# Attention, two feed-forward stages and one core: a new table of task times for the list scheduler of the attention stage

## The chip, the cores and the metric

One core of a Trainium2 chip runs the whole program in one launch. The metric is the device time of one execution, in microseconds. TensorE (PE) does the matmuls and the transposes, VectorE (DVE), ScalarE (ACT) and GpSimd (POOL) the arithmetic between them, SyncE (SP) issues most DMAs, ACT's queue a few.

## The reference, cut to what matters

```python
p_packed = sm_attn(p, k, v)            # 32 packed rows per head attend to 576 keys
out = sm_attn(q, p_packed, p_packed)   # 576 queries per head attend to the 32 packed rows
x = out.transpose(0, 2, 1, 3).reshape(B * S, H * D)      # 4608 tokens x 512
x = moe(x)     # 8 experts, the best one per token: relu(x @ w1[e]) @ w2[e], times its gate
return moe2(x) # h = x @ w_in (512 x 2048); silu(h) @ w_out
```

There are 8 batches of 8 heads, 576 positions and a head size of 64; everything is float32.

## The kernel before, in words

The program has three stages one after the other: `attention` (which also computes the first expert layer of batch 0), `experts`, and `ffn`. The change touches only the order of the first.

`attention` writes no instruction directly. It describes operations (`Sched.op`): an engine, a cost in the model, what it reads and writes, and the task that it belongs to. `Sched.run` then sorts all operations by the time of their task in the table `TIMES` (plus the operation's place within the task), looks at the first `window` operations of what is left, and takes the one that can start soonest by the model's costs; on a tie the one that stands earlier. It does this until nothing is left, and emits the instructions in that order. Each engine runs its own instructions in exactly the order emitted. DMA issues on SP keep the order in which `attention` names them; their rank is below everything.

The tasks are named by a letter, a batch b and a part:

- `k` (b, t): transposes of the keys (`ktp`, L1624, and `krp`, L1611) and of the packed rows (`ptp`, L1598), then the scores `s1p` (L1638, L1643), maximum on DVE, exponent on ACT.
- `p` (b, t): the exponents are transposed (`e1p`, `e1rp`, L1665 and L1671), multiplied by the values (`ppp`, L1690), scaled, transposed again (`pptp`, L1698); `mp` (L1716, L1719) are small products for the router.
- `q` (b, r): queries are transposed (`qtp`, L1736, which reads the tile `qm`), their scores are `s2p` (L1753), then the softmax on DVE, ACT and POOL. r is 0 or 1; part 2 of an odd batch is the rest of two batches (`qs`, L1819, L1828).
- `x` (b, r): the weights are transposed (`a2p`, L1776, L1849), stored to DRAM from ACT's queue, and multiplied with `mp` for the router's logits (`xp`, L1790, L1860).
- `r` (u): the routing of two batches, with the small product `cnt` (L389, L390).
- `m`: the first expert layer of batch 0. Part 0 loads the expert's weights `w1c` (2 MiB, L467) and the stored attention `af`; parts 1 and 2 multiply the packed rows with them (`m0p`, L506); parts 3 to 10 are eight products `a0p` (L541), each followed by a relu on ACT (L544) and the low half on DVE (L548). `m0p` and `a0p` all write the one PSUM buffer with the tag `s1`, which the scores `s1p` use before them: a product can start only when ACT and DVE have read the one before.
- `d`: a copy on POOL that doubles the packed rows.

Loads of keys (`km` 1 MiB, `kr` 128 KiB), values (`vm`, `vr`) and queries (`qm`, and `qs` for odd batches) have two buffers each. So the load of batch b's queries waits until all transposes of batch b-2's queries are done, and as SP's order is fixed, every load behind it in SP's queue waits with it. SP's order after the first batches is: keys of b+2, queries of b+1, values of b+2, packed rows of b+3, keys of b+3 and so on; the 2 MiB of `w1c` come behind the last queries.

When the last operation of the stage has been emitted, `experts` follows, whose first PE instruction is at L600; L620 is its second layer.

## Time and profile before

| | us |
|---|---|
| median of 3 runs | 1213.74 (1213.04 to 1214.96) |
| the profiled execution, its own time | 1214.78 |
| its span | 1212.9 |
| PE busy | 1173.9 (97% of the span) |
| DVE, ACT, POOL busy | 876.9, 526.4, 146.9 |
| attention stage, until PE reaches L600 | 0 to 178.37 |

The span is the time from the first to the last instruction that the profiler saw; some 2 us of the execution lie around it. A time in a row is counted from the start of the span. A busy PE is a PE that has a matmul in flight; as matmuls overlap, the next row's start says more about the length of a group than its own duration does.

### The profile page before, as it was taken

To read this page: it belongs to the slowest core of one execution; us is meant where nothing else is said; L and a number is where in the kernel's file an instruction comes from. 1 tells how busy PE (TensorE), PEld (TensorE's weight loads), DVE (VectorE), ACT (ScalarE), POOL (GpSimd) and SP (SyncE) were. 2 spreads that over 40 slices of the span, in tenths; PEclk is the share of its full clock that TensorE was granted. 3 is DMA by queue.
4 is the path that set the end of the run, shared out by engine and by line. 5 is a ranking of instruction groups with operands and counts; after the bars stand their busy time and mean duration, and the time that the engine had idled before them with its cause. 6 is when DMAs were issued, how large, how long until landed. Compare 5 with 4: busy or idle time off the path is not lost.

```text
span 1212.9 us, 24417 instructions
## 1 busy us (share of the span) xinstructions
PE 1173.9 (97%) x9548; PEld 1034.1 (85%) x9549; DVE 876.9 (72%) x1560; ACT 526.4 (43%) x911; POOL 146.9 (12%) x259
## 2 busy tenths in 40 slices
PE   8788899999999999999999999999999999999998
PEld 7676679999989998978878878889998888888887
DVE  5475877886897883586765585634878888888886
ACT  4565652333343233464445354434643333333342
POOL 3222220221132432100000000002000000000000
PEclk9999999999999999999999999999999999999999
DMA  9979657569668965576876745788855657575652
GB/s 260 258 222 264 213 184 248 189 245 336 248 233 297 341 209 164 168 231 194 312 253 200 233 142 147 229 260 259 273 212 173 189 176 216 161 221 164 208 145 49
DMA packets 228313, 264.62 MB, mean 218 GB/s; under 512 B 32024, under 2 KB 181784, under 8 KB 227680
## 3 DMA queue, kind: packets, MB, share of 16 engines
q1 hardware_dynamic: 213192, 230.66, 59.2%
q0 software_dynamic: 8048, 27.53, 8.4%
q10 hardware_dynamic: 6952, 4.80, 1.3%
q8 instruction: 77, 1.26, 0.4%
q14 instruction: 44, 0.36, 0.1%
HBM read 175.26 MB, written 87.69 MB: 217 GB/s over the span
## 4 chain that ended last, share of the span: by engine, by line
PE 56%; DVE 3%; issue 1%; ACT 1%; DMA 0%; SPq 0%; DVEq 0%; ACTq 0%
PE p L1202 17%; PE p L1200 10%; PE p L906 8%; PE p L908 8%; PE p L907 8%; PE ps L620 2%; DVE x L899 1%; PE p L1205 1%; PE p L1204 1%; PE ps L541 1%; DVE raw L899 0%; DMA raw<-y_d 0%; DVE mh L899 0%; DMA c_d<-x 0%; DVE y L899 0%
## 5 line engine op out<-in xcount | busy, mean ns | idle before, releaser
L899 DVE TENSOR_TENSOR x<-p,x 128x512 f32<-128x512 f32 (+1 forms) x148 | 90.2, 619 | 58.8 <-PE p L908 52.8
L940 ACT ACTIVATE x<-x 128x512 f32<-128x512 f32 (+1 forms) x111 | 66.7, 603 | 137.5 <-DVE x L899 125.5
L620 PE MATMUL ps<-hkm,w2s 128*128 128x288 f32 x768 | 123.5, 296 | 0.0
L620 PEld LDWEIGHTS ps<-hkm,w2s 128*128 128x128 f32 x768 | 108.5, 188 | 5.9 <-DVE cu L678 1.7
L541 PE MATMUL ps<-at,mh 128*128 128x288 f32 x672 | 93.1, 297 | 4.2 <-PEq L735 2.1
L541 PEld LDWEIGHTS ps<-at,mh 128*128 128x128 f32 x672 | 90.5, 188 | 5.4 <-issue 3.5
L1202 PE MATMUL p<-x,x 128*128 128x512 f32 x332 | 90.4, 394 | 0.0
L620 PE MATMUL ps<-hvm,w2s 128*128 128x288 f32 x448 | 85.3, 295 | 0.0
L1202 PEld LDWEIGHTS p<-x,x 128*128 128x128 f32 x332 | 62.7, 189 | 10.8
L620 PEld LDWEIGHTS ps<-hvm,w2s 128*128 128x128 f32 x448 | 68.3, 188 | 0.1
L899 DVE TENSOR_TENSOR x<-p,y 128x512 f32<-128x512 f32 (+1 forms) x57 | 33.1, 581 | 42.8 <-PE p L908 39.1
L899 DVE TENSOR_TENSOR y<-p,y 128x256 f32<-128x256 f32 (+1 forms) x71 | 34.5, 485 | 35.4 <-PE p L1200 27.3
L1169 ACT CAST x<-rawe 128x1024 fp32r<-128x1024 f32 x35 | 36.4, 1051 | 49.5 <-DVE rawe L899 49.5
L620 PE MATMUL ps<-hqm,w2s 128*128 128x288 f32 x320 | 52.7, 294 | 0.0
L544 ACT ACTIVATE hkm<-ps 128x576 fp32r<-128x576 f32 x42 | 27.3, 652 | 55.7 <-PE ps L541 50.0
L630 ACT COPY yb<-ps 128x576 f32<-128x576 f32 x20 | 12.8, 642 | 88.3 <-PE ps L620 84.8
L1202 PE MATMUL p<-t,x 128*128 128x512 f32 x166 | 51.1, 389 | 0.0
L1187 POOL DMA_DIRECT2D x<-c_d x14 | 12.1, 865 | 319.8 <-DMA x<-c_d 223.1
L620 PEld LDWEIGHTS ps<-hqm,w2s 128*128 128x128 f32 x320 | 46.0, 188 | 0.0
L906 PE MATMUL p<-x,t 128*128 128x512 f32 x112 | 43.9, 392 | 1.5 <-DVE x L899 1.0
L591 DVE TENSOR_TENSOR w2s<-w2c,w2s 128x1024 fp32r<-128x1024 f32 x32 | 40.1, 1252 | 7.2 <-ACT w2s L588 7.2
L1222 ACT COPY raw<-p 128x256 f32<-128x256 f32 x18 | 6.7, 373 | 86.4 <-PE p L1200 86.4
(442 smaller groups left out, 3235.1 us busy)
## 6 DMA issues: line engine op xcount, KB each, us to landing
c_d<-x SPq DMA_DIRECT2D x136, 256.0 KB, 2.9
raww1c<-c_d SPq DMA_DIRECT2D x36, 512.0 KB, 6.1
rawe<-c_d SPq DMA_DIRECT2D x36, 512.0 KB, 5.0
w1c<-in_moe_w_dram SPq DMA_DIRECT2D x32, 512.0 KB, 10.4
w2c<-in_moe_w_dram SPq DMA_DIRECT2D x32, 512.0 KB, 4.0
y_d<-yb SPq DMA_DIRECT2D x36, 288.0 KB, 2.1
raw<-y_d SPq DMA_DIRECT2D x36, 256.0 KB, 4.8
x<-c_d SPq DMA_DIRECT2D x18, 512.0 KB, 3.9
```

The lines of the kernel that those rows point to most:

```text
L541: PE.matmul(out=a[:, i, 0:H2], lhsT=mh[x][:, t, f], rhs=at[y][:, t, n], start=t == x == y == 0, stop=t == x == 1, skip_group_check=True)
L544: self.nc.scalar.activation(out=self.hT(0, m).rearrange("p (i n) -> p i n", i=2), in_=a[:, :, 0:S // 2], func=ACTF.Relu)
L591: DVE.tensor_tensor(out=l, in0=w2c[c % 2], in1=h.bitcast(F32), op=ALU.subtract)
L620: PE.matmul(out=a[:, i, 0:H2], lhsT=w[:, k, :], rhs=hT(z, k, n), start=w is h and k == z == 0, stop=w is l and k == 7, skip_group_check=True)
L899: eng.tensor_tensor(out=o, in0=x, in1=y, op=op)
L906: PE.matmul(out=o, lhsT=h, rhs=a[0][k][:, 0:n], start=start and k == 0, stop=False, skip_group_check=True)
L907: PE.matmul(out=o, lhsT=h, rhs=a[1][k][:, 0:n], start=False, stop=False, skip_group_check=True)
L908: PE.matmul(out=o, lhsT=l, rhs=a[0][k][:, 0:n], start=False, stop=k == 1, skip_group_check=True)
L940: ACT.activation(out=y, in_=x, func=ACTF.Silu)
L1169: ACT.copy(out=slots[s % R][0], in_=src)
L1200: PE.matmul(out=o, lhsT=l[:, g], rhs=x[:, 0:256], start=False, stop=stop and g == gs[-1], skip_group_check=True)
L1202: PE.matmul(out=bank, lhsT=h[:, g], rhs=x, start=first and g == gs[0], stop=False, skip_group_check=True)
```

## The change

The table `TIMES` is replaced by another one (all 95 entries have other values), and the window of the list scheduler goes from 300 to 600 operations. The model's costs, latencies and its rate for transfers (the divisor 310.0 in `run`) are the same in both files. No operation is added or removed; each engine has the same instructions as before, apart from how runs of them are grouped.

```diff
 TIMES = {
-    ('p', 3, 0): -2360329, ('x', 0, 0): -2355626, ('k', 0, 0): -2266171, ('m', 0, 11): -2135614, ('p', 1, 0): -2135064, ('x', 1, 1): -1898965,
...
-    ('x', 7, 0): -109829, ('k', 6, 0): -69273, ('d', 4, 0): -34552, ('q', 6, 0): -30408, ('m', 0, 8): 83284, ('m', 0, 0): 125359,
...
+    ('x', 3, 2): -1927255, ('p', 5, 1): -1896583, ('p', 0, 1): -1886500, ('x', 7, 2): -1790949, ('x', 4, 1): -1780171, ('x', 6, 1): -1743462,
...
+    ('q', 1, 0): 2056181, ('d', 5, 0): 2094409, ('k', 4, 0): 2408114, ('m', 0, 5): 2408567, ('x', 3, 0): 2619733,
 }
...
-    def run(self, times, window=300):
+    def run(self, times, window=600):
```

SP's rows are the same before and after, word for word. On PE, DVE, ACT and POOL the order within the attention stage differs; behind L600 nothing differs.

The first place is on PE, at the last transposes of batch 1's queries (tile `qm_291`). Before, three of these four groups stand further up, and the last one stands here, between the keys of batch 3 (`km_590`) and the scores of those keys:

```order
L1624 MATMUL ktp_1084<-ident_62,km_590 128x128 x4
L1624 MATMUL ktp_1094<-ident_62,km_590 128x128 x4
L1736 MATMUL qtp_1102<-ident_62,qm_291 128x128 x4
L1849 MATMUL a2p_1113<-ident_62,a2s_994 128x128 x2
L1638 MATMUL s1p_1120<-kT_979,pT_951 32x256 x4
L1638 MATMUL s1p_1120<-kT_988,pT_951 32x256 x4
L1643 MATMUL s1p_1120<-kTr_1068,e1_148 32x32 x8
L1716 MATMUL mp_1144<-ppT_1077 32x32 x4
```

Now its first part (`q`, 1, 0) stands here, behind the keys and scores of batch 4 and behind all four transposes of batch 2's queries; the tile `qm_1517`, in the last row, is batch 3's queries:

```order
L1736 MATMUL qtp_1473<-ident_62,qm_291 128x128 x4
L1753 MATMUL s2p_1479<-e1_148,qT_1160 64x2x32 x8
L1753 MATMUL s2p_1479<-e1_148,qT_1169 64x2x32 x8
L1736 MATMUL qtp_1503<-ident_62,qm_291 128x128 x4
L1665 MATMUL e1p_1511<-ident_62,e1_1501 128x128 x4
L1671 MATMUL e1rp_1522<-ident_62,e1_1501 64x128
L1753 MATMUL s2p_1540<-e1_148,qT_1474 64x2x32 x8
L1753 MATMUL s2p_1540<-e1_148,qT_1504 64x2x32 x8
L1776 MATMUL a2p_1563<-ident_62,a2s_1531 128x128 x4
L1790 MATMUL xp_1585<-e0_147,a2f_1564 64x72 x16
L1776 MATMUL a2p_1610<-ident_62,a2s_1582 128x128 x4
L1736 MATMUL qtp_1623<-ident_62,qm_1517 128x128 x4
```

All that stood ahead of the last `qm_291` group before still does, and 34 more groups of PE stand ahead of it. The load of `qm_1517` goes into the buffer of `qm_291`.

The second place is on PE too, at the first product with the expert's weights (`m0p`). Before:

```order
L1819 MATMUL qtp<-ident,qs 128x128 x4
L1790 MATMUL xp<-e_147,a2f 64x72 x16
L1753 MATMUL s2p<-e_148,qT 64x2x32 x16
L1665 MATMUL e1p<-ident,e_2512 128x128 x4
L1736 MATMUL qtp<-ident,qm 128x128 x4
L1671 MATMUL e1rp<-ident,e_2512 64x128
L1665 MATMUL e1p<-ident,e_2697 128x128 x4
L506 MATMUL m0p<-w1c,pp_125 32x512 x8
L1776 MATMUL a2p<-ident,a2s 128x128 x4
```

and now, where the last values (`ppp`) of batch 7 and its queries stand ahead of it:

```order
L1690 MATMUL ppp<-vm,e1T 32x64 x16
L1690 MATMUL ppp<-vr,e1Tr 32x64 x4
L1819 MATMUL qtp<-ident,qs 128x128 x4
L1736 MATMUL qtp<-ident,qm 128x128 x4
L1716 MATMUL mp<-ppT 32x32 x4
L1719 MATMUL mp<-e_148,ppT 32x8 x4
L1753 MATMUL s2p<-e_148,qT 64x2x32 x16
L1698 MATMUL pptp<-ident,ppd 128x128
L1736 MATMUL qtp<-ident,qm 128x128 x8
L506 MATMUL m0p<-w1c,pp_125 32x512 x8
L1776 MATMUL a2p<-ident,a2s 128x128 x4
```

Thirteen groups that stood behind the first `m0p` now stand ahead of it, and one small one (`mp`) went the other way.

The third place is the end of PE's work in the stage, up to L600 (`at`, `mh` are the operands of `a0p`; `cnt` is the last routing product). Before, the last of the eight `a0p` (three rows each) has `xp` and `a2p` ahead of it and `cnt` behind it:

```order
L1790 MATMUL xp<-e_147,a2f 64x72 x16
L1776 MATMUL a2p<-ident,a2s 128x128 x4
L1790 MATMUL xp<-e_147,a2f 64x72 x16
L541 MATMUL a0p<-at_139,mh_142 128x288 x4
L541 MATMUL a0p<-at_140,mh_142 128x288 x4
L541 MATMUL a0p<-at_139,mh_143 128x288 x4
L389 LDWEIGHTS ones
L389 MATMUL cnt<-oh,ones 128x8
```

and now, with the last rows of that `cnt` at the top, two `a0p` stand back to back in front of L600:

```order
L389 LDWEIGHTS ones
L389 MATMUL cnt<-oh,ones 128x8
L390 LDWEIGHTS ones
L390 MATMUL cnt<-oh,ones 128x8
L541 MATMUL a0p<-at_139,mh_142 128x288 x4
L541 MATMUL a0p<-at_140,mh_142 128x288 x4
L541 MATMUL a0p<-at_139,mh_143 128x288 x4
L541 MATMUL a0p<-at_139,mh_142 128x288 x4
L541 MATMUL a0p<-at_140,mh_142 128x288 x4
L541 MATMUL a0p<-at_139,mh_143 128x288 x4
L600 MATMUL ps_3519<-w1c,pp_126 32x512
```

## Rows read from the trace of the kernel before

**Rows 1.** the page, part 1: busy us (share of the span) xinstructions
```profile
PE 1173.9 (97%) x9548; PEld 1034.1 (85%) x9549; DVE 876.9 (72%) x1560; ACT 526.4 (43%) x911; POOL 146.9 (12%) x259
```

**Rows 2.** stretches: us, busy us (instructions) by engine, granted clock, DMA share, GB/s
```profile
0.00:57.10 57.10, 47.04 (x886) 37.93 (x887) 28.77 (x104) 28.15 (x61) 17.21 (x61) 0.98 0.98 263
57.10:138.50 81.40, 71.24 (x1687) 56.00 (x1685) 54.92 (x180) 50.36 (x121) 19.60 (x46) 0.99 0.84 240
138.50:178.40 39.90, 36.99 (x691) 30.37 (x691) 31.32 (x90) 24.78 (x64) 8.65 (x14) 1.00 0.58 182
178.40:198.40 20.00, 20.00 (x165) 17.82 (x163) 18.33 (x52) 7.98 (x10) 0.00 (x0) 1.00 0.54 174
```

**Rows 3.** SP's queue in order of time: start us, us, DMA
```profile
57.10 0.38 SPq L1523 DMA_DIRECT2D qm<-in_q_dram  x1
...
121.21 3.87 SPq L467 DMA_DIRECT2D w1c<-in_moe_w_dram  x4
```

**Rows 4.** the DMA queue's waits, 0 to 150 us: total us, times, longest
```profile
SPq L1523 <- PE qtp L1736: 17.7, 3, 10.9
```

**Rows 5.** PE in order of time: start us, us, instructions [idle before <-releaser]
```profile
56.01 1.06 PE L1736 MATMUL qtp<-ident,qm 128*128 128x128 f32 x4
...
66.62 0.47 PE L1860 MATMUL xp<-e,a2f 64*64 64x72 f32 x13 [2.44 <-issue]
...
86.17 1.15 PE L1753 MATMUL s2p<-e,qT 128*64 128x64 f32 x32
87.25 1.53 PE L1736 MATMUL qtp<-ident,qm 128*128 128x128 f32 x12
88.71 0.66 PE L1638 MATMUL s1p<-kT,pT 64*32 64x256 f32 x16
...
89.57 0.66 PE L1736 MATMUL qtp<-ident,qm 128*128 128x128 f32 x4
90.06 0.60 PE L1665 MATMUL e1p<-ident,e 128*128 128x128 f32 x4
...
90.70 0.73 PE L1790 MATMUL xp<-e,a2f 64*64 64x72 f32 x32
91.36 1.09 PE L1624 MATMUL ktp<-ident,km 128*128 128x128 f32 x8
92.29 0.38 PE L1598 MATMUL ptp<-ident,pd 128*128 128x128 f32 x2
```

**Rows 6.** the transfers of 57.1 to 138.5 us, all queues
```profile
DMA packets 23946, 19.53 MB, mean 240 GB/s; under 512 B 9210, under 2 KB 23290, under 8 KB 23930
```

**Rows 7.** a stretch in which SP hardly waits, columns as in rows 2
```profile
104.00:128.00 24.00, 19.71 (x513) 15.47 (x512) 14.51 (x48) 11.96 (x28) 6.44 (x15) 1.00 1.07 298
```

**Rows 8.** PE's waits, 0 to 138.5 us: total us, times, longest
```profile
PE ppp L1690 <- issue: 4.1, 2, 2.2
...
PE ptp L1598 <- issue: 0.5, 1, 0.5
```

**Rows 9.** PE in order of time, the first expert layer up to L600
```profile
138.53 1.92 PE L506 MATMUL m0p<-w1c,pp 128*32 128x512 f32 x16
...
148.46 1.81 PE L541 MATMUL a0p<-at,mh 128*128 128x288 f32 x12
...
151.95 1.86 PE L541 MATMUL a0p<-at,mh 128*128 128x288 f32 x12
...
178.37 2.88 PE L600 MATMUL ps<-w1c,pp 64*32 64x512 f32 x32
```

**Rows 10.** DVE in order of time, behind the first m0p and the first a0p
```profile
141.56 1.22 DVE L510 TENSOR_TENSOR mh<-m0p,mh 128x1024 fp32r<-128x1024 f32 x1 [0.21 <-ACT mh L509]
...
150.99 0.76 DVE L548 SCALAR_TENSOR_TENSOR hqm<-a0p,hkm 128x576 fp32r<-128x576 f32 x1
```

**Rows 11.** two microseconds in which the granted clock fell, columns as in rows 2
```profile
56.00:58.00 2.00, 2.00 (x24) 1.32 (x22) 0.00 (x0) 1.42 (x3) 1.74 (x4) 0.50 0.48 105
```

**Rows 12.** the page, part 3: queue, packets, MB, share of 16 engines
```profile
q8 instruction: 77, 1.26, 0.4%
```

## The prediction

> **What bounds the kernel now.** I read the page first: PE is busy 97% of the span [rows 1], so whatever delays PE delays the end. Then the stretches: the attention stage, which alone is changed, ends at 178.4 us, and in the 20 us behind it PE is busy all of them [rows 2]. So a shift of the stage's end goes through to the end of the program, one for one; no later wait is there to swallow it, or it would show as idle PE.

> Within the stage there are three parts. Up to 57.1 us the DMA engines are full (share 0.98) and PE idles 10.1 us. From 57.1 to 138.5 us PE idles another 10.2 us, with a DMA share of 0.84. From 138.5 us, where the first product with the expert's weights (`m0p`) starts, to L600 it idles 2.9 us [rows 2]. Of the idle before 138.5 us, "issue" is the largest cause: six rows from `ppp` 4.1 to `ptp` 0.5, 12.5 us together [rows 8]; one such stall, of 2.44 us, lies in the middle of an `xp` group [rows 5]. PE hardly waits for a load. It is SP that waits: three times for the transposes of queries, 17.7 us in all [rows 4].

> The last part has a bound of its own, the one PSUM buffer `s1`. The first `m0p` starts at 138.53 and its low half leaves DVE at 141.56 + 1.22 = 142.78, so a round takes some 4.4 us with the hand-over. The first `a0p` starts at 148.46, DVE is done at 150.99 + 0.76 = 151.75, and the next starts at 151.95: a round of 3.5 us [rows 9, 10]. Two rounds of 4.4, seven of 3.5 and the last product's 1.9 are 35.2 us, whatever stands between. Before, the part takes 178.37 - 138.53 = 39.84 us [rows 9].

> **The change part by part.** No operation goes or comes, so the sum is one of work moved past a bound, and of waits.

> *Work ahead of the first `m0p`.* Thirteen groups move ahead of it. By starts of successive rows [rows 5]: an `s2p` takes 87.25 - 86.17 = 1.08, a `qtp` of four 1.46 / 3 = 0.49, an `s1p` 89.57 - 88.71 = 0.86, an `e1p` with its `e1rp` 0.64, an `xp` 0.66, a `ktp` of four 0.93 / 2 = 0.47. I put a `ppp` at the 0.86 of the `s1p` (as many small matmuls) and an `a2p` at the 0.47 of the `ktp` (four transposes as well); both are estimates. One `s2p`, two `ppp`, three `qtp`, two `xp` and two `a2p` are 1.08 + 1.72 + 1.46 + 1.32 + 0.94 = 6.5; `cnt`, `pptp` and one `e1rp` add some 0.65, and an `mp` of 0.16 leaves. With idle time unchanged the first `m0p` starts 7.0 us later, at 145.5. **+7.0.**

> *The chain behind it.* The moved work stood between the rounds of `s1` before, and is missing there now. From the first `m0p` on the new order, at the same durations, has PE work of 3.6, 4.1, 4.0, 4.1 and then only 2.7, 2.6, 2.4, 2.0 and 1.7 us from one start to the next, so most rounds run at their bound: 4.4 + 4.4 + 4.0 + 4.1 + 5 x 3.5 + 1.9 = 36.3 us. Before, the same sum (work or bound, whichever is longer: 5.0, 4.6, 3.5, 3.8, 3.5, 3.8, 3.7, 3.5, 3.5, then 2.1 with `cnt`) is 37.0, and the part took 39.84, 2.8 more in ten rounds. With 1.7 of that for after (one hand-over, that of the last `cnt`, is gone from the end) the part takes 38.0. **-1.8**, between -3.5 (nothing lost in the rounds) and -1.0 (2.5 lost). So PE now idles some 9 us here where it idled 2.9; this is where the saved work goes.

> *The hole in the loads.* The load of batch 3's queries is freed by the last transposes of batch 1's. Before, these start at 56.01, and the load goes out at 57.10 [rows 3, 5]. Now 34 more groups stand ahead of them: four `s1p`, `ktp` and `qtp` each, two `ppp` and `s2p`, three `e1p` with `e1rp`, an `xp` and an `a2p` come to 14.2 us, ten small ones to 2.4, about 16.5 together. So the load, and everything behind it in SP's queue, goes out at 57.1 + 16.5 = 73.6 at the earliest, and at 76.0 with the idle share of that stretch (81.40 us for 71.24 busy, so 18.9 for 16.5) [rows 2]. Meanwhile nearly nothing is moved. Then 19.53 MB are to come until the expert's weights are there, as in the same stretch before [rows 6]. No SP wait stands in between any more: all later buffers are free long before SP's turn comes. At the 298 GB/s of a stretch in which the queue is full [rows 7] that takes 65.5 us, to 141.5; at the 263 GB/s of the first 57 us [rows 2] 74.3, to 150.3. PE comes to `m0p` at 145.5 by its own work. So the weights come 4 us in time, or 4.8 late.

> On the way PE will wait for loads, which it hardly did. Batch 3's queries are used behind only 3.3 us of work (`e1p` with `e1rp`, `s2p`, `xp`, two `a2p`), and 1 MiB takes 3.5 at 298 GB/s with nothing added for the way: 0.2 or more, I take 2. The keys of batch 6 are needed 20.6 us of work after that load's issue (the 31 groups between, at the same durations), with some 7.2 MB of loads and 0.8 MB of stores to move until then, which is 27 us: with the idle that PE has anyhow, 3 more. **+5** for both, 0 to +6.

> *Idle that goes.* In the hole the DMA engines are free, and "issue" stalls lie in stretches with a busy DMA: the 2.44 at 64 to 66.6 us then lies in the hole, and of the other 10.1 us a quarter may go as the early order is another one. **-5**, between 0 and -12.5 (all of [rows 8]).

> Sum: +7.0 - 1.8 + 5 - 5 = **+5.2 us**. Against the profiled execution, 1214.78 us, that is 1220.0; that execution lay 1.0 above the median of the runs, 1213.74, so on the scale of the medians I predict **1218.9 us**.

> [...]

> The 77 packets of the instruction queue hold 16.4 KB each [rows 12]. [...]

> **The rivals.**

> *Faster: the idle falls by more than the order costs.* The place is PE between 30 and 138 us, the price is 12.5 us of issue stalls [rows 8] and the 1 of the low clock [rows 11]. If 8 of these go and the queries of batch 3 come in time (5 less), the first `m0p` starts at 145.5 - 8 = 137.5, and the end comes at -1.0 - 1.8 = -2.8: 1211. It decides from 7.6 us less idle than forecast net of waits. For it: the stalls are the largest idle, and they are tied to traffic. Against: once the hole is over, the traffic is denser than before.

> *No change.* The stalls shrink by 5 more than I take, or the chain runs at its bound of 36.3: the sum is between -2 and +2, 1213.7. The DMA side then has the weights there at 141.5, 3 us behind the old start of `m0p`, and the chain gives these back.

> *Slower still: the loads become the bound.* At 263 GB/s the weights come at 150.3, PE waits for them whatever it has saved, and the end is +11.8 - 1.8 = +10: 1223.7. For it: in the first stretch, with full DMA engines, no more was moved. Against: from 104 to 128 us 298 were.

> *The change doesn't do what it says.* The rate in the model is 310 in both files; if the table was searched with another, the order emitted here need not be the one that was found good. That changes no number, as I read the order that is emitted.

> **How the numbers follow.** A measurement of this kernel tells 0.2%, 2.4 us, from no change. Forecast (+2.4 to +8): 0.46; loads as bound (above +8): 0.12; no change: 0.20; faster: 0.22. So slower 0.58. The forecast's own range is 1216 to 1222; for 8 in 10 I need the better half of the faster case and most of the load case: 1209.5 to 1224.5.

> **What would show it.** In the new profile: the third long wait of SP for `qtp` ends near 76 us and lasts 18 or more; the DMA share is near 0 ahead of it and near 1 for the 60 us behind it; PE waits some microseconds for `qm` or `km`; the first `m0p` starts near 145.5 and L600 38 us later, with idle PE between the last `a0p`. If L600 starts before 176, the forecast is wrong; if `m0p` starts late but L600 doesn't, the chain was mis-sized; if it starts early, the idle was.

## The result and the profile after

The kernel after takes 1228.49 us (median of 5 runs, 1225.74 to 1230.68), the kernel before, in runs on the same chip, 1213.74 (1211.24 to 1215.51): a ratio of 1.0122, 95% interval 1.010 to 1.0144. In a second set of runs the same two gave 1.0094 (1.0058 to 1.0129). So it is slower, as forecast, but by 11 to 15 us and not by 5.

The profiled execution of after took 1230.68 us, 15.9 more than that of before; its span is 1228.1. The page's first part, as in [rows 1]:

```profile
PE 1182.8 (96%) x9548; PEld 1040.4 (85%) x9549; DVE 876.4 (71%) x1560; ACT 526.9 (43%) x911; POOL 148.7 (12%) x259
```

PE has the same 9548 instructions and is busy 8.9 us longer: the same matmuls ran slower. The other 6.3 us of the span are idle. The stretches, with the columns of [rows 2], but cut at the first `m0p` and at L600:

```profile
0.00:60.00 60.00, 50.81 (x923) 39.59 (x925) 29.75 (x110) 28.70 (x63) 16.42 (x57) 0.91 0.91 251
60.00:149.65 89.65, 78.68 (x1842) 62.49 (x1840) 60.70 (x198) 55.46 (x134) 22.10 (x52) 0.98 0.77 224
149.65:190.51 40.86, 32.67 (x498) 25.96 (x498) 25.28 (x74) 18.50 (x47) 8.03 (x12) 0.93 0.57 186
```

Look at the granted clock, the third figure from the end: 0.91, 0.98 and 0.93, where before had 0.98, 0.99 and 1.00 (its stretches end at 57.1, 138.5 and 178.4 us). And look at the idle time, the stretch less PE's busy time: 9.2 + 11.0 = 20.2 us up to the first `m0p`, the same as before (10.1 + 10.2), and 8.2 behind it, where before had 2.9.

PE in order of time, the rows that answer to [rows 9], with the last five `a0p`:

```profile
149.65 1.92 PE L506 MATMUL m0p<-w1c,pp 128*32 128x512 f32 x16
...
171.50 1.83 PE L541 MATMUL a0p<-at,mh 128*128 128x288 f32 x12 [1.30 <-DVE lg_all L1803]
...
175.25 1.81 PE L541 MATMUL a0p<-at,mh 128*128 128x288 f32 x12 [0.74 <-DVE hqm L548]
...
179.52 1.81 PE L541 MATMUL a0p<-at,mh 128*128 128x288 f32 x12 [1.80 <-DVE mx L378]
...
183.44 2.36 PE L541 MATMUL a0p<-at,mh 128*128 128x288 f32 x12 [1.87 <-DVE hqm L548]
187.33 3.25 PE L541 MATMUL a0p<-at,mh 128*128 128x288 f32 x12 [1.53 <-DVE hqm L548]
190.51 2.30 PE L600 MATMUL ps<-w1c,pp 64*32 64x512 f32 x32
```

The first `m0p` is 11.1 us later than before, L600 12.1. Each of the last five `a0p` waits for the DVE read of the product before (L548). Two rows name another DVE instruction, but there too L548 ends some 0.15 us ahead of the `a0p`, as it does ahead of that at 175.25:

```profile
170.61 0.75 DVE L548 SCALAR_TENSOR_TENSOR hqm<-a0p,hkm 128x576 fp32r<-128x576 f32 x1
174.35 0.75 DVE L548 SCALAR_TENSOR_TENSOR hqm<-a0p,hvm 128x576 fp32r<-128x576 f32 x1
178.62 0.75 DVE L548 SCALAR_TENSOR_TENSOR hqm<-a0p,hkm 128x576 fp32r<-128x576 f32 x1
```

The last two `a0p` are slow themselves (2.36 and 3.25 us instead of 1.81). They ran at the low clock. Three stretches that hold it, columns as in [rows 11]:

```profile
47.00:55.00 8.00, 6.91 (x115) 5.21 (x114) 2.86 (x14) 1.18 (x3) 1.74 (x6) 0.57 0.96 274
74.00:80.00 6.00, 5.90 (x102) 4.56 (x103) 3.59 (x13) 2.93 (x8) 0.82 (x3) 0.72 0.57 155
184.00:192.00 8.00, 6.47 (x46) 4.84 (x52) 1.46 (x2) 2.04 (x3) 0.00 (x0) 0.57 0.01 2
```

I count half of PE's busy time as lost where the clock is at 0.50. Taken microsecond by microsecond (busy time x (1 - granted clock)) that gives 6.8 us ahead of the first `m0p` and 2.3 behind it; in the profile of before 1.7 and 0. What remains of busy time is PE's work at full clock. So L600 splits into three (us; from here on called idle, slow and work):

```
                 idle to m0p  idle to L600  slow to m0p  slow to L600  work    L600
before               20.2          2.9          1.7          0.0       153.6   178.37
before, again        19.0          2.9          3.4          0.0       153.4   178.71
after                20.2          8.2          6.8          2.3       153.2   190.51
after, again         20.9          8.2          7.9          2.0       152.7   191.66
```

The work is the same within 0.9 us, so the way of counting holds. On the mean of two profiles each, L600 comes 12.5 us later: 6.2 of idle time, 6.9 of low clock, 0.6 back. (The second profiles are from the experiments below.)

### The profile page after: what moved, and what is told of

Same layout as the page of the kernel before. It is cut to its first block, busy times and chain, and to the rows that moved or that the text cites. A ratio compares the mean times of both kernels' runs of the same rounds, so it can differ in the third digit from the quotient of the medians.

```text
span 1228.1 us, 24417 instructions
## 1 busy us (share of the span) xinstructions
PE 1182.8 (96%) x9548; PEld 1040.4 (85%) x9549; DVE 876.4 (71%) x1560; ACT 526.9 (43%) x911; POOL 148.7 (12%) x259
## 4 chain that ended last, share of the span: by engine, by line
PE 56%; DVE 3%; issue 1%; ACT 1%; DMA 0%; SPq 0%; DVEq 0%; ACTq 0%
PE p L1202 17%; PE p L1200 10%; PE p L906 8%; PE p L908 8%; PE p L907 8%; PE ps L620 2%; DVE x L899 1%; PE p L1205 1%; PE p L1204 1%; PE ps L541 1%; DVE raw L899 0%; DMA raw<-y_d 0%; DVE mh L899 0%; DMA c_d<-x 0%; DVE y L899 0%
## 5 line engine op out<-in xcount | busy, mean ns | idle before, releaser
L541 PE MATMUL ps<-at,mh 128*128 128x288 f32 x672 | 95.6, 302 | 4.4 <-PEq L735 2.2
L541 PEld LDWEIGHTS ps<-at,mh 128*128 128x128 f32 x672 | 93.2, 193 | 5.4 <-issue 3.9
L899 DVE TENSOR_TENSOR x<-p,y 128x512 f32<-128x512 f32 (+1 forms) x57 | 33.1, 581 | 42.7 <-PE p L908 38.9
L1187 POOL DMA_DIRECT2D x<-c_d x14 | 12.1, 865 | 320.0 <-DMA x<-c_d 223.4
```

Of the source, the lines that this page charges most:

```text
L541: PE.matmul(out=a[:, i, 0:H2], lhsT=mh[x][:, t, f], rhs=at[y][:, t, n], start=t == x == y == 0, stop=t == x == 1, skip_group_check=True)
L899: eng.tensor_tensor(out=o, in0=x, in1=y, op=op)
```

## The experiments

All are built on the order that the scheduler leaves, just before it is emitted; line numbers stay. `task` and `eng` are an operation's task and engine. Ratios are to runs of the kernel before in the same set.

```
run                          median   ratio (95%)              idle m0p/L600  slow m0p/L600   L600
e1  layer 40 earlier         1231.24  1.0136 (1.0102, 1.017)    20.5 / 12.5     7.8 / 0.9    193.85
e2  before, layer 35 later   1225.87  1.0075 (1.0048, 1.0103)   20.2 / 11.1     6.7 / 2.6    193.63
e3  46 fillers, tail         1225.00  1.0085 (1.0059, 1.0111)   20.3 /  0.9     6.7 / 0.0    191.74
e4  batch 1's queries later  1225.69  1.0091 (1.0061, 1.012)    20.4 /  8.2    11.3 / 0.0    192.94
e5  two buffers              1224.28  1.009  (1.0061, 1.0119)   21.3 /  7.0     3.1 / 0.0    185.09
e6  before, two buffers      1215.50  1.0013 (0.9988, 1.0038)   18.7 /  3.4     5.0 / 0.0    179.84
e7  layer 19 earlier         1228.58  1.0111 (1.0085, 1.0136)   18.8 / 10.3     9.9 / 0.2    193.15
e8  31 fillers, tail         1226.28  1.0107 (1.008, 1.0135)    20.2 /  1.3     8.1 / 0.0    189.70
e9  early after, late before 1225.93  1.0098 (1.0065, 1.0131)   23.2 /  3.0     5.9 / 0.0    184.90
e10 early before, late after 1230.77  1.0144 (1.0114, 1.0173)   21.0 /  8.2     9.0 / 2.0    191.51
e11 after to m0p, then before 1226.60 1.0095 (1.0067, 1.0123)   20.7 /  7.4     8.2 / 2.2    190.09
e12 after, again             1227.22  1.0094 (1.0058, 1.0129)   20.9 /  8.2     7.9 / 2.0    191.66
e13 18 fillers, early        1228.61  1.0102 (1.0081, 1.0124)   20.9 /  9.2     8.4 / 2.6    198.68
e14 49 fillers, both         1225.85  1.0083 (1.0062, 1.0104)   20.1 /  1.9     8.4 / 0.0    195.41
e15 before, again            1216.64  (one run)                 19.0 /  2.9     3.4 / 0.0    178.71
```

Idle, slow and L600 are of the one profiled execution. The work is 151.3 to 153.9 in every run without fillers.

**Where the first layer stands: e1, e7, e2.**

```diff
+        order = [o for _, o in sorted(enumerate(order), key=lambda x: x[0] + (-40 - 0.5 if <task m, not SP> else 0))]
```

> The kernel after, with the whole first layer's stage (its m0p, a0p and what hangs on them on TensorE, VectorE and ScalarE) emitted 40 operations earlier, so that 7.4 us less of the attention's PE work stands ahead of the first m0p; nothing else moves. My theory (place of the stage plus low clock): first m0p near 142.0 instead of 149.65, L600 near 183 instead of 190.5, and a time near 1221 us, 6 to 8 below the kernel after. It leaves the low-clock stretches at 37 to 55 and 75 to 79 us where they are. Rival (the work has to be done anyway, so where the stage stands in it is neutral): L600 and the time unchanged, near 1228, since what is moved behind the stage makes the stage longer by the same 7 us. Rival (the weights' loads bound the stage): the first m0p then waits for w1c and moves by less than half of the 7.4 us.

The first `m0p` came at 142.54, as expected. L600 came at 193.85, and the time didn't fall: my theory was wrong here, and the rival (the place is neutral) nearly right. PE at the end of that stage:

```profile
182.14 1.86 PE L541 MATMUL a0p<-at,mh 128*128 128x288 f32 x12 [0.88 <-DVE hqm L548]
183.84 0.38 PE L1849 MATMUL a2p<-ident,a2s 128*128 128x128 f32 x2
186.35 0.48 PE L1860 MATMUL xp<-e,a2f 64*64 64x72 f32 x16 [2.13 <-DVE lg_all L1803]
188.57 0.66 PE L1776 MATMUL a2p<-ident,a2s 128*128 128x128 f32 x4 [1.73 <-POOL a2s L1768]
189.90 1.24 PE L1790 MATMUL xp<-e,a2f 64*64 64x72 f32 x32 [0.68 <-ACT a2f L1779]
193.51 0.25 PE L389 MATMUL cnt<-oh,ones 128*128 128x8 f16 x4 [2.37 <-DVE oh L382]
```

Now the layer is done at 184, and the attention's own last chain (softmax, transposes, router) runs bare for 9.5 us. There are two tails, and each needs the other's work between its links.

> The kernel after, with the first layer's stage emitted 19 operations earlier, half of the first such run (in which the a0p's ended at 184 and the attention's last chain, softmax, transposes, router, at 193.8; in the kernel after it is 190.5 and 181.4). Theory 1 (two tails share TensorE, and idle is least where they end together): both tails end near 187.4, so L600 starts some 3 us earlier than in the kernel after, with 4 to 6 us idle behind the first m0p instead of 8.2, and the time is 1224 to 1226. Theory 3 (the place of the stage is neutral): L600 near 190.5 and 1228, as at 0 and at 40.

Half the shift gave 10.3 us idle and L600 at 193.15, no better: the last `cnt` stood at 192.81, since the `a0p` put ahead of the last router work delay it. So the two tails don't simply trade one against the other, as theory 1 has it.

> The kernel before, with the first layer's stage emitted 35 operations later, so that 5.4 us more of the attention's PE work stands ahead of the first m0p (the place that it has in the kernel after, nearly), with the loads and the attention in the order of before. My theory: first m0p near 143.9, L600 4 to 6 us later than 178.4, the time 1218 to 1220; where the a0p's then stand in bare PE time, low clock in the tail comes on top, as in the kernel after. Rival (neutral place): 1213.7, no change. Rival (the whole loss comes from the moved place): 1224 or more, as much as the kernel after loses.

The same done to before costs 9 to 10 us (ratio and medians), more than I expected: the time is that of the second rival. Its profile has 11.1 us idle behind the first `m0p`: `cnt` waits 2.81 us for DVE, then three `a0p` stand alone.

**The halves of the change: e9, e10, e11.** `ORDER` lists the operations: the first ones in one kernel's order, the rest in the other's.

```diff
+ORDER = [...]
...
+        order = [self.ops[i] for i in ORDER]
```

> Half of the change: the first 647 of the stage's 872 operations in the order of the kernel after (102.7 us of TensorE work, with its loads' holes and its early waits), the others in the order of the kernel before (the first m0p behind 113.2 us of work; before 112.1, after 119.0). Theory 1 (the order's price lies behind the first m0p, as idle that grows from 2.9 to 8.2 us; the low clock comes on top and changes from one execution to the next): idle behind the first m0p is 3 to 4 us, L600 starts at 180 to 184, by the low clock ahead of it, and the time is 1216 to 1220. Rival (the early part, with its order of loads and waits, is what costs): the time is 1224 or more, as of the kernel after.

> The other half: the first 627 operations in the order of the kernel before (101.7 us of TensorE work), the others in that of the kernel after (the first m0p behind 119.0 us of work, and the last a0p's without work between them). Theory 1: idle behind the first m0p is 8 to 9 us, with low clock among the last a0p's, L600 starts at 186 to 190, the time is 1221 to 1226. Rival (the early part costs): 1214 to 1217, as of the kernel before.

> The order of the kernel after up to 8 operations short of its first m0p (117.8 us of TensorE work), then the order of before: the thirteen groups still stand ahead of the first m0p, the two m0p and the first a0p follow each other with under 2 us of work between them, and from there on the a0p's have the work between them that they have in the kernel before. By the rounds on the one buffer (4.4 us for an m0p) the part from the first m0p to L600 takes 4.4 + 4.4 + 29.9 = 38.7 us, of which 7 to 8 are idle: the place of the thirteen groups alone gives the loss, L600 at 186 to 189, time 1222 to 1225. Rival (the spacing of the last a0p's is the loss, not the groups ahead of the first m0p): idle of 3 to 5 us, L600 at 181 to 184, time 1217 to 1220.

The two halves of e9, ahead of and behind the first `m0p`, and of e10:

```profile
0.00:146.09 146.09, 122.89 (x2607) 97.63 (x2608) 84.77 (x287) 79.65 (x187) 37.75 (x107) 0.95 0.84 238
146.09:184.90 38.81, 35.80 (x655) 29.45 (x654) 30.30 (x88) 23.25 (x59) 7.61 (x13) 1.00 0.58 182
```

```profile
0.00:150.92 150.92, 129.88 (x2764) 103.78 (x2765) 91.74 (x307) 84.39 (x197) 38.40 (x109) 0.93 0.83 233
150.92:191.51 40.59, 32.36 (x498) 25.67 (x497) 25.32 (x74) 18.49 (x47) 8.01 (x12) 0.93 0.56 188
```

The idle time behind the first `m0p` goes with the late half, as expected: 38.81 - 35.80 = 3.0 us with that of before, 8.2 with that of after. The times are not those that I expected: e9 took what the rival said, 11.5 us more than before though its tail is as in before (3 us more idle time ahead of the `m0p`, and low clock), and e10, with 16 us more, lies above both kernels. The halves don't add up to the change. Each joint brings waits of its own (e9: 2.00 us at 136 us, e10: 1.03, 0.89 and 1.61 us at 122 to 130). In e11 the a0p's are spaced as in before; its 7.4 us of idle time are nearly those of after, and the part from the first `m0p` to L600 takes 40.2 us (38.0 without its low clock; expected 38.7). So the groups ahead of the first `m0p` are enough for the idle time, and the spacing of the last `a0p` isn't needed for it.

**The one buffer: e5, e6.**

```diff
+            if o.eng == "PE" and o.task and o.task[0] == "m" and o.task[2] in (2, 10, 5):
+                <the product's tile>.tag = "x"
```

> The kernel after, the same order on every engine; three of the ten products of the first layer (the first m0p, the a0p at 179.5 us and the last a0p) write the other PSUM buffer, with the tag x, which the router's xp has between them, so they don't wait until DVE has read the product before. Theory 1 (what comes late is idle TensorE time plus low clock, and the idle behind the first m0p, 8.2 us against 2.9 before, comes from the round on one buffer once no other work is left to fill it): the waits of 1.9 and 1.5 us ahead of the last two a0p's go and with them the low clock there (another 1.9 us), L600 starts at 185 to 187 instead of 190.5, the time is 1223 to 1225. Theory 2 (the last softmax and routing on DVE end the stage, as they did where the layer was moved ahead): the a0p's wait for DVE all the same, L600 stays at 189 to 191 and the time at 1227 to 1229.

> The control: the kernel before with the same edit (the first m0p, the second and the fourth a0p of its order write the buffer with the tag x). Theory 1: here the rounds have other work between them and TensorE idles only 2.9 us behind the first m0p, so at most 1 us is to be had: 1213 to 1216, no change that can be told. A gain as large as that of the kernel after with the same edit would speak against theory 1.

L600 came at 185.09 and the control didn't move, both as theory 1 has it. But the sum of causes was another: idle behind the `m0p` fell only from 8.2 to 7.0, low clock by 2.3 there and by 3.7 ahead of it, where nothing had been changed. So the edit is worth about 1 us, and the rest is clock. The waits of the `a0p` themselves did fall, from 7.4 to 3.6 us, but other instructions now wait behind the first layer's products:

```profile
PE xp L1790 <- DVE mh L510: 1.7, 1, 1.7
PE ps L600 <- DVE hvm L548: 1.5, 1, 1.5
```

So this shows what the edit is worth, and not what the rounds on one buffer cost.

**The low clock: e3, e8, e13, e14, e4.** The fillers are products of the identity with itself into a PSUM tile that nobody reads.

```diff
+        fill = {9: 8, 7: 8, 10: 8, 8: 14, 5: 14}
...
+            if o.eng == "PE" and o.task and o.task[0] == "m" and o.task[2] in fill:
+                self.filler(fill[o.task[2]])
```

> The kernel after with 46 matmuls of 128 columns that compute nothing that is used (a spare PSUM tile), ahead of the last five a0p's, 8 to 14 before each, where TensorE stood idle for 0.7 to 1.9 us each and the granted clock fell to 0.50 at 184 to 192 us. My theory: the idle time between the a0p's is what brought the low clock; with it filled the clock stays at 1.00 there, the a0p's at 183 and 187 us take 1.9 us and not 2.4 and 3.3, L600 starts about 2 us earlier, and the time is about 1226.5. Rival (the low clock comes from something else, such as what TensorE did before 180 us, or its power): the clock falls all the same, and the fillers make the chain 1 to 3 us longer.

> The kernel after with 31 filler matmuls that compute nothing that is used, cut to the length of the gaps (6, 3, 8, 7 and 7 ahead of the last five a0p's; the first such run had 46 and made the tail longer, 42.3 us from the first m0p to L600, while the clock stayed at 1.00). Theory 1: the clock stays at 1.00 in the tail, the last five rounds are those of the full clock (4.2, 3.8, 4.3, 3.6 and 3.5 us), L600 starts 39 us behind the first m0p, and the time is 1223 to 1224.5. Rival: with shorter fillers the low clock is back, or L600 is no earlier than with the 46.

PE at the end of the stage with the shorter fillers (L1900 is the filler):

```profile
184.56 1.83 PE L541 MATMUL a0p<-at,mh 128*128 128x288 f32 x12 [0.21 <-DVE hqm L548]
186.24 1.72 PE L1900 MATMUL s2p<-ident 128*128 128x128 f32 x14
187.93 1.84 PE L541 MATMUL a0p<-at,mh 128*128 128x288 f32 x12
189.70 1.95 PE L600 MATMUL ps<-w1c,pp 64*32 64x512 f32 x32
```

No low clock in the tail in either; the last `a0p` take 1.83 and 1.84 us, and from the first `m0p` to L600 it is 38.9 us with the shorter fillers, as expected (40.86 in after). In e3 the longer ones made it 42.36, and L600 was not earlier, though I had expected that. The medians, 1225.0 and 1226.3, lie below those of after, but their intervals overlap with it. Over all profiles with this tail, low clock came in four of the five without fillers (after, e10, e12, e13, but not e4) and in none of the three with them (e3, e8, e14). That makes it likely that the fillers hold the clock; the gain in time isn't shown.

> The kernel after with 18 filler matmuls of 128 columns that compute nothing that is used, ahead of three TensorE instructions that wait at 36 to 102 us: 7 ahead of the transposes of batch 1's rest of the queries (they wait 1.2 to 1.7 us for their load), 4 and 7 ahead of the a2p and the xp at 99 and 101 us (0.7 and 1.3 us for POOL and ACT). Theory 1 (such waits, which the new order brings, are what sets off part of the low clock): no low clock at 37 to 41 and 100 to 107 us, what is left lies at 47 and 74 us behind issue stalls; low clock ahead of the first m0p costs 4 to 5 us instead of 6.7 to 8.1, and the time is 1.5 to 3 us below the kernel after, 1224.5 to 1226. Rival (the fillers only add work, the dips move elsewhere): 1228 to 1230.

> The fillers of the run before and those cut to the gaps ahead of the last five a0p's together, 49 matmuls that compute nothing that is used. Theory 1: L600 at 186 to 188, the mean clock of the runs at 0.993 or above, the time 1221 to 1224; what is left over the kernel before is the idle time of its order (now filled, 5 to 6 us). Rival: 1226 or more, as with one of the two.

In e13 the dips (stretches of low clock) at 47 and 74 us stayed and that at 100 us went, but one at 34 to 38 came ahead of the first filler, and a filler itself waited 1.92 us for DVE to free its PSUM tile (at 103.91). The time was the rival's: idle ahead of the `m0p` stayed at 20.9 us, so the fillers' work (127.1 us with them, 122.7 in after) came on top instead of into gaps. e14 has the mean clock that was expected (0.9943), but neither the time nor L600, for the same reason.

> The kernel after with the transposes of batch 1's queries and their copies emitted 20 places later, behind TensorE work that is ready, so that TensorE doesn't wait for the load of these queries at 35 to 38 us (0.64 and 1.17 us in the trace), ahead of the low clock at 37 to 42 us. My theory: the waits of 1.8 us go and with them the first dip of the clock (which costs about 1.7 us at half speed for 4 to 5 us of window), so the first m0p comes 2 to 3.5 us earlier and the time is 1225 to 1226.5. Rival: the stall moves to the next instruction, the dip stays, and the time doesn't change.

The wait for the load went, and an issue stall of 1.68 us stood there in its place (38.85 us), with low clock from 40 us; the rival was right about the stall. The time is within the spread of after.

**The kernels again: e12, e15.**

> The kernel after, unchanged, to see what of it comes back in another execution. Theory 1: idle ahead of the first m0p 20 to 21 us and behind it 8 to 9, as in the first profile, but the stretches of low clock lie elsewhere and their price ahead of the first m0p is anything from 3 to 11 us; time 1226 to 1230. Rival (the low clock is fixed by the order): the same stretches at 37, 48, 75, 184, 351 and 478 us.

> The kernel before, unchanged, for a second profile: idle time as in the first (20 us ahead of the first m0p, 3 behind it), low clock of another size in other places, 1.7 to 5 us ahead of the first m0p as in the first profile and in that of before with two buffers; L600 at 178 to 182.

The same instructions in after, again; two stretches of it, and the second one in the first profile of after:

```profile
47.00:55.00 8.00, 7.58 (x134) 5.88 (x134) 3.74 (x15) 1.41 (x3) 1.74 (x6) 0.62 1.13 304
100.00:108.00 8.00, 6.92 (x111) 5.34 (x113) 3.59 (x15) 5.41 (x12) 0.00 (x0) 0.57 0.60 144
```

```profile
100.00:108.00 8.00, 6.32 (x173) 4.67 (x170) 4.60 (x16) 5.15 (x12) 0.00 (x0) 1.00 0.73 189
```

The rival of e12 was nearer: the stretches at 47, 74, 186, 353 and 476 us came back, that at 37 didn't, and one at 100 is new. e15 came as expected; it has two low stretches behind L600 as well, at 341 and 464 us, about as far behind it as those at 351 and 478 us in after, so these two don't belong to the change.

Five profiles have after's order up to the first `m0p` (after, e12, e3, e8 and e5, whose edit bears on the first layer alone). In all five PE stalls at the same `ppp` at 46 to 48 us (2.35 to 2.94 us, issue), and the clock falls to 0.50 behind it. At the same `mp` at 73 to 74 us all five stall (1.4 to 1.9), and the clock falls in four. Behind the waits of 0.7 and 1.3 us at 97 to 101 us it fell in three. The low clock ahead of the `m0p` costs 6.7 to 8.1 us in four of them and 3.1 in e5; in the three profiles with before's order (before, e15, e6) 1.7 to 5.0. The two ranges overlap, so the profiles alone don't show that the order brings more of it.

The timed runs do: the mean granted clock is 0.9949 over 52 runs of before and 0.9904 over 11 of after. Over all 148 runs, with a level for each kernel, a clock lower by 0.001 goes with 0.97 us more (a straight line, scatter 1.8 us). Of the 12.3 us between the means that is 4.4 us for the clock, and 7.9 at equal clock. At equal clock e2 lies 8.6 us above before, e10 7.7, e5 6.8, e11 6.3 and e9 5.9, each give or take 0.8. So the later place of the first layer, put alone into the order of before (e2), costs as much as the whole change apart from the clock.

## Why the prediction was wrong, step by step

*PE sets the end, one for one.* Held: 12.1 us at L600, 15.2 at the end of the span. The 3.1 between are low clock at 351 to 356 and 478 to 482 us, which the second profile of before has too.

*+7.0, work ahead of the first `m0p`.* Held in size: work up to it went from 116.6 to 122.7, so +6.1. It is no price by itself. As PE's work is fixed (152.7 to 153.6 us up to L600 in the four profiles above), moved work costs only what PE idles for lack of it later; the prediction's own remark that PE "now idles some 9 us here where it idled 2.9" was the better form of the sum, and 8.2 was measured. e11 shows that these groups alone bring most of it (7.4 us idle).

*-1.8, the chain behind it.* The part took 40.86 us instead of 39.84, so +1.0; without its 2.3 us of low clock it is 38.6, so -1.3. The term held at full clock.

*+5, waits for loads.* The place failed, at "The load of batch 3's queries is freed by the last transposes of batch 1's". Which of the two buffers a load gets follows the order that is emitted. In the new order all of batch 2's queries are transposed ahead of the last of batch 1's, so batch 3's load (`qm_1517`) gets the buffer of batch 2's and not, as the section on the change has it, that of `qm_291`, which goes to batch 4. It goes out behind batch 2's transposes. PE, with the transposes of batch 2 and the last of batch 1, then SP, with the loads of batches 3 and 4:

```profile
60.14 1.98 PE L1736 MATMUL qtp<-ident,qm 128*128 128x128 f32 x16
...
79.21 0.66 PE L1736 MATMUL qtp<-ident,qm 128*128 128x128 f32 x4
```

```profile
62.15 0.37 SPq L1523 DMA_DIRECT2D qm<-in_q_dram  x1
...
79.89 0.38 SPq L1523 DMA_DIRECT2D qm<-in_q_dram  x1
...
123.69 3.23 SPq L467 DMA_DIRECT2D w1c<-in_moe_w_dram  x4
```

So batch 3's load was 5 us later than before [rows 3] and not 16.5 or more, and no long hole came; the weights went out at 123.69, 2.5 us later. SP's waits for `qtp` are four now, where [rows 4] had three:

```profile
SPq L1523 <- PE qtp L1736: 20.4, 4, 8.9
```

*-5, idle that goes.* The issue stalls up to the first `m0p` shrank by about what was taken, from the 12.5 of [rows 8] to 6.9, but not for the reason given, as there was no hole:

```profile
PE ppp L1690 <- issue: 4.5, 2, 2.4
PE e1p L1665 <- ACT kT L1629: 1.6, 2, 1.2
PE mp L1719 <- issue: 1.6, 1, 1.6
...
PE xp L1860 <- ACT a2f L1852: 1.3, 1, 1.3
PE qtp L1819 <- DMA qs<-in_q_dram: 1.2, 1, 1.2
...
PE xp L1790 <- issue: 0.8, 1, 0.8
...
PE qtp L1736 <- DMA qm<-in_q_dram: 0.6, 1, 0.6
```

The idle time stayed at 20.2, so other waits took their place: 1.8 us for loads of queries (before: 0.8 us, for keys), the rest for ACT, DVE and POOL. The +5 and the -5 cancelled as written, for another reason; that is luck.

A rival ties these stalls to traffic, but they don't need full DMA engines: one in the profile of before, from 50.9 to 53.0 us, lies at a DMA share of 0.36. Their places are tied to the number of instructions that PE has run. Up to the stall that ends at 45.1 us in before, at 48.1 in after and at 48.3 in e13, PE had run the same 723 matmuls (the first count of each row). What it ran next was an `s2p` in before, a `ppp` in after, and in e13, with seven fillers ahead (14 matmuls in the trace), a `ppp` that stands 14 matmuls earlier in the order:

```profile
0.00:45.00 45.00, 37.33 (x723) 29.58 (x725) 22.37 (x85) 23.45 (x52) 13.81 (x51) 1.00 1.00 264
0.00:47.50 47.50, 39.31 (x723) 30.92 (x725) 22.31 (x81) 23.84 (x53) 13.63 (x50) 0.96 0.97 265
0.00:48.00 48.00, 40.46 (x723) 33.17 (x725) 22.30 (x81) 23.85 (x53) 13.58 (x50) 0.96 0.99 272
```

In all seventeen profiles, every issue stall over 0.5 us ahead of the first `m0p` comes at 345, 471, 597, 723, 850, 1102, 1230, 1608, 1987, 2113, 2238, 2366 or 2493 matmuls, give or take two: steps of 125 to 128, or of two or three times that. (Five of just 0.50 us, at 474, don't.) Which instruction such a place falls on changes with the order, and PE doesn't stall at each of them (in before at 597, 723, 850, 1102, 1987, 2113 and 2366, in after at 723, 1230, 1608 and 2493); where the places are stays. PE's 19,097 matmuls and weight loads [rows 1] are 248 for each of the 77 packets of [rows 12], and 126 matmuls with their weight loads are 252: an estimate, which takes all of these packets as PE's. What PE waits for at these places, no run shows; and as no hole came, none shows what a hole would do to the stalls.

*The low clock, left out of the sum.* This is the step that failed. The sum has no term for it; the prediction prices it once, in the faster rival, as "the 1 of the low clock" [rows 11]. In the profile it is 9.1 us up to L600 against 1.7: 5.1 more ahead of the first `m0p`, 2.3 behind it. At full clock the terms make +6.1 - 1.3 + 0 = +4.8, close to the +5.2 of the sum. With the clock it is 12.1. The timed runs put 4.4 us on the clock; without these the median of after would be some 1224.1 (an estimate), just inside the range that the prediction gave. The low clock came behind a wait for a load (1.17 us for `qs`, at 37 us), but also behind issue stalls (2.35 us at 48 and 1.60 us at 74 us) and among waits for DVE (1.87 us ahead of 183.44 us, 1.53 us ahead of 187.33).

*The rivals.* Loads as bound: no, the first `m0p` waited for nothing. Faster, no change: no. That the table was searched with another rate was not tried.

What stays open: how the loss divides. By two profiles each it is 6.2 us of idle time and 6.9 of low clock up to L600; by the timed runs 4.4 of clock and 7.9 of the rest. The profiled executions of after had a mean clock of 0.988 and 0.987, below the 0.9904 of its runs, and the first of before 0.998, above its 0.9949; so the profiles put too much on the clock, and the 4.4 is the better figure. Of the 7.9, 5.3 are the idle time behind the first `m0p`; where the rest lies isn't shown. Nor is why the new order brings more low clock, and why one stall is followed by it and another isn't: behind the 2.44 us of [rows 5] the clock stayed, behind 2.1 and 2.2 us at that same `xp` in e10 and e15 it fell, and behind 2.1 us there in e6 it stayed. No order or edit tried here beats the kernel before.

## What to carry to other kernels

When only an order changes, the busy engine's work is fixed (here within 0.9 us of 153.6): write the end of the stage as work + idle + slow clock, and forecast the idle time from every chain that loses its cover, on both sides of the move (e1 and e7 show the price of seeing one side only). Give the clock a term of its own, some 2 us for each new wait behind which it may fall (an estimate: one dip ahead of the first `m0p` cost 1.4 to 4.0 us in the profiles here). One profile is one draw: compare its low clock with the mean clock of the timed runs before taking it as the kernel's own.

## What the runs showed of the hardware that was not expected

PE's issue stalls come back at the same numbers of matmuls in all seventeen profiles, whatever the order: that at 723 took 1.23 us in the profile of before and 2.35, 2.79, 2.80, 2.79 and 2.94 in five with after's order, and all 83 that took over 0.5 us ahead of the first `m0p` came at the places above. So they go with the number of matmuls that PE has run, though they wait for nothing that the profile shows.
